# Late chunks in pairs, fewer transposes on TensorE, and seven products for four output blocks of a recurrent attention kernel with an MLP

## The chip, the core and the metric

The kernel runs on one core of a Trainium2 chip. A core has five engines with queues of their own, each in order: TensorE (PE in the profile, its weight loads PEld), VectorE (DVE), ScalarE (ACT), GpSimd (POOL) and SyncE (SP), which here issues nearly all DMAs. TensorE writes to PSUM, eight banks of 128 partitions by 512 float32; the others work between PSUM and SBUF, the on-chip memory of 128 partitions, GpSimd on SBUF alone. The metric is the device time of one execution in microseconds, the median over runs; smaller is better.

## What is computed

Four batches, eight heads, 768 tokens, head size 48. Each head keeps a 48 x 48 state that decays per key channel; the output of all heads (3072 tokens by 384) goes through two matrix products with a leaky ReLU between them.

```python
for t in range(S):
    cur = einsum('bhd,bhe->bhde', u[None] * kt, vt)
    y[:, :, t] = einsum('bhd,bhde->bhe', rt, state + cur)
    state = wt[:, :, :, None] * state + einsum('bhd,bhe->bhde', kt, vt)
x = y.transpose(0, 2, 1, 3).reshape(B * S, H * D)
h = x @ w_in                     # 384 -> 2048
g = np.maximum(0.01 * h, h)
out = g @ w_out                  # 2048 -> 384
```

Inputs and output are float32; the kernel computes its products in bfloat16 with float32 sums.

## The kernel before

The 3072 tokens are 24 chunks of 128. In a chunk the recurrence is made parallel: cumulative sums of log w by a triangular matrix product, their exponentials into r and k (`rk`), both transposed (`rkT`), scores k against r, a mask, masked scores against v, and the state of the previous chunk against r. The bonus with u is r u k summed per head, times v (`vs`). The result y of a chunk is transposed into `xT`, whose columns are the tokens.

The first four chunks are two pairs (function `pair`), 256 tokens each, with two consecutive tokens in one partition, so that a row of a load has 96 floats (per head) instead of 48. The other 20 are single chunks (`single`), each with four loads (L701), a log (L711), one cumulative sum on TensorE (L717) and per-head-pair totals (L720), sums with the log on DVE (L729), exponentials on ACT (L743, L747, L738 for the totals), products on DVE (L405), transposes, scores (L858, eight matmuls that contract over the 48 rows of one head, two heads in the two halves of the array), two masks on DVE (L788), state sums (L798, four matmuls of 96 columns), a scaled state on GpSimd (L775), the new state on DVE (L813), and y: four matmuls from the state (L824) and eight from the masked scores (L829) into one bank, plus the bonus on DVE (L478). `run` takes one or two chunks (`MERGED`) and puts their scores into one step.

A transpose of r and k is either eight matmuls against the identity (L416) with two evacuations on DVE or ACT (L421, L423), or one DMA transpose from SP (`RK_DMA` lists 13 chunks). The transpose of y is three matmuls (L464) and a copy (L469, L471), or a DMA transpose (`Y_DMA` lists 8 chunks).

The MLP goes over blocks of one or two chunks: 16 groups of 128 columns of w_in, three matmuls each (L901), the leaky ReLU on ACT into g (L916, 512 columns at a time), and 16 accumulating matmuls of 384 columns per chunk (L928), a copy on DVE or ACT (L939, L941) and a store (L945).

The order of everything is a written plan. Each step is added to a `Plan` with the engines that may run it, an assumed cost, a priority, the steps it follows and the buffers it reads or takes; `Plan.order` then plays the steps through in assumed time, gives each an engine and a buffer, and the kernel emits the instructions in that order. `RANK` shifts priorities of single steps, `FORCE` fixes engines; limits bound how many PSUM banks a kind of buffer holds at once (`hp` for L901's results 2, `op` for L928's 2). A log must wait until the first L901 step of the chunk `LEAD` before it. In the first 24 us of assumed time gaps of TensorE are filled with matmuls of zeros (L970).

## Time and profile before

| | us |
|---|---|
| runs | 182.0, 183.03, 183.03 |
| median | 183.03 |
| the profiled execution | 181.38 |
| its span, first to last instruction | 179.6 |

The profile comes from that one execution. Busy time of an engine is the union of its instructions; for TensorE the durations of successive matmuls overlap, so one instruction's duration is more than what it adds. The groups of instructions by line give busy time, mean duration in ns of one, and the idle time before them with what ended it. The chain of waits follows the work back from the last instruction to what released it at each step.

The shares of work on TensorE, by line (count, busy us):

| line | what | count | busy us |
|---|---|---|---|
| L901 | x times w_in | 720 | 73.3 |
| L928 | g times w_out | 384 | 73.4 |
| L416 | transposes of r and k | 88 | 7.7 |
| L829 | masked scores times v | 160 | 7.2 |
| L858 | scores | 160 | 6.7 |
| L824 | state into y | 72 | 6.0 |
| L798 | state sums | 64 | 5.3 |
| L464 | transposes of y | 48 | 5.3 |

### The profile page before, as it was taken

Reading aid. Unit: us, or ns where it says so; the run is one execution under the profiler, and the core shown is the slowest. Engines: PE = TensorE matmul, PEld = TensorE weight load, DVE = VectorE, ACT = ScalarE, POOL = GpSimd, SP = SyncE. Lnnn points to the kernel's source line nnn. Section 1 sums busy time; section 2 is a strip of 40 time slices with the busy share of each in tenths; the row PEclk is TensorE's granted clock in tenths of the full one; section 3 lists DMA queues with packets and bytes.
Section 4 is the critical chain, followed back from the end, with each engine's and each line's share of the span. In section 5 each row is a group of like instructions: output and inputs, shape, how many; then the busy total and the mean of one; then the engine's idle time right before and its main releaser. Section 6 shows DMA issues by size and latency. Waiting matters only on the chain.

```text
span 179.6 us, 5197 instructions
## 1 busy us (share of the span) xinstructions
PE 171.6 (96%) x2036; PEld 129.8 (72%) x2037; DVE 115.0 (64%) x231; ACT 115.3 (64%) x253; POOL 102.5 (57%) x138
## 2 busy tenths in 40 slices
PE   7798999999999999999999999999999999999991
PEld 2466888867778788877788767787788786787850
DVE  7699764289789898559677558397468297241102
ACT  2678968855867788884489774485486664652610
POOL 5999632574897686877469854667165665100000
PEclk9999999999999999999999999999999999999998
DMA  5999999998999999999999989999899996600112
GB/s 141 261 283 316 370 376 364 187 199 199 231 191 224 180 229 134 184 213 173 185 181 223 212 179 223 153 215 175 152 254 170 220 163 134 167 9 19 47 44 88
DMA packets 116571, 34.43 MB, mean 192 GB/s; under 512 B 109121, under 2 KB 115778, under 8 KB 116546
## 3 DMA queue, kind: packets, MB, share of 16 engines
q1 hardware_dynamic: 116544, 34.09, 95.8%
q8 instruction: 16, 0.26, 0.7%
q14 instruction: 9, 0.07, 0.1%
q10 hardware_dynamic: 2, 0.00, 0.0%
HBM read 25.17 MB, written 4.72 MB: 166 GB/s over the span
## 4 chain that ended last, share of the span: by engine, by line
PE 77%; DMA 11%; DVE 4%; ACT 2%; issue 2%; SPq 1%; POOL 0%; DVEq 0%; ACTq 0%
PE ps L901 35%; PE ps L928 28%; DMA in<-in_r_dram 3%; DMA in<-in_v_dram 3%; DMA in<-in_w_dram 2%; PE ps L858 2%; DMA xT<-y 2%; PE ps L829 2%; PE ps L717 2%; PE ps L824 2%; PE ps L416 2%; DVE rk L405 2%; PE ps L798 1%; PE ps L464 1%; DVE m L636 1%
## 5 line engine op out<-in xcount | busy, mean ns | idle before, releaser
L901 PE MATMUL ps<-xT,w_in_b 128*128 128x256 bf16 (+1 forms) x720 | 73.3, 251 | 0.4 <-ACT xT L471 0.2
L928 PE MATMUL ps<-w_out_b,g 128*128 128x384 bf16 x384 | 73.4, 326 | 0.0
L916 ACT ACTIVATE g<-ps 128x512 bf16<-128x512 f32 x96 | 56.8, 597 | 25.4 <-PE ps L901 23.2
L901 PEld LDWEIGHTS <-w_in_b 128*128 128x128 bf16 x720 | 57.8, 98 | 9.9 <-issue 0.7
L928 PEld LDWEIGHTS <-g 128*128 128x128 bf16 x384 | 35.2, 98 | 17.3
L405 DVE TENSOR_TENSOR rk<-in,ps 128x384 bf16<-128x384 f32 x46 | 24.5, 548 | 9.9 <-ACT ps L743 6.5
L435 POOL TENSOR_TENSOR ru<-in,ub 128x384 f32<-128x384 f32 x24 | 23.9, 1001 | 9.6 <-DMA in<-in_k_dram 7.6
L788 DVE TENSOR_TENSOR m<-ps,maskb 128x512 bf16<-128x512 f32 x40 | 25.1, 683 | 5.3 <-PE ps L858 5.3
L439 POOL TENSOR_TENSOR ru<-ru,in 128x384 f32<-128x384 f32 x24 | 24.6, 1027 | 3.0 <-DMA in<-in_r_dram 2.4
L775 POOL TENSOR_TENSOR sb<-s,a 128x384 bf16<-128x384 f32 x18 | 15.0, 831 | 16.8 <-ACT a L738 16.8
L447 POOL TENSOR_TENSOR vs<-in,dg 128x384 f32<-128x384 f32 x20 | 16.6, 830 | 9.1 <-DVE dg L443 8.4
L729 DVE TENSOR_TENSOR ci<-ps,lw 128x384 f32<-128x384 f32 x20 | 11.1, 555 | 9.7 <-PE ps L720 4.5
L939 DVE COPY o<-ps 128x384 f32<-128x384 f32 x10 | 5.6, 555 | 15.6 <-PE ps L928 15.4
L443 DVE TENSOR_REDUCE dg<-ru 128x8 f32<-128x384 f32 x24 | 12.9, 544 | 2.1 <-POOL ru L439 2.1
L478 DVE TENSOR_TENSOR y<-ps,vs 128x384 bf16<-128x384 f32 x20 | 11.1, 553 | 3.2 <-PE ps L829 2.6
L455 POOL CAST vb<-in 128x384 bf16<-128x384 f32 x24 | 12.0, 504 | 1.5 <-DMA in<-in_v_dram 1.4
L711 ACT ACTIVATE lw<-in 128x384 bf16<-128x384 f32 x20 | 10.4, 522 | 2.9 <-DMA in<-in_w_dram 2.9
L743 ACT ACTIVATE ps<-ps 128x384 f32<-128x384 f32 x20 | 9.6, 481 | 4.1 <-DVE ci L729 3.6
L738 ACT ACTIVATE a<-ps 64x4 f32<-64x4 f32 x36 | 6.0, 167 | 7.7 <-DVE ci L729 5.1
L813 DVE TENSOR_TENSOR s<-ps,sb 128x384 f32<-128x384 f32 x14 | 7.7, 552 | 3.8 <-PE ps L798 2.7
L747 ACT ACTIVATE ps<-ci 128x384 f32<-128x384 f32 x20 | 9.8, 491 | 0.0
L941 ACT COPY o<-ps 128x384 f32<-128x384 f32 x14 | 6.7, 479 | 4.2 <-PE ps L928 4.0
(90 smaller groups left out, 176.2 us busy)
## 6 DMA issues: line engine op xcount, KB each, us to landing
out_dram<-o SPq DMA_DIRECT2D x24, 192.0 KB, 3.7
in<-in_w_dram SPq DMA_DIRECT2D x20, 192.0 KB, 4.2
in<-in_k_dram SPq DMA_DIRECT2D x20, 192.0 KB, 4.2
in<-in_r_dram SPq DMA_DIRECT2D x20, 192.0 KB, 4.0
in<-in_v_dram SPq DMA_DIRECT2D x20, 192.0 KB, 4.0
in<-in_moe_w_out_dram SPq DMA_DIRECT2D x4, 768.0 KB, 12.1
in<-in_moe_w_in_dram SPq DMA_DIRECT2D x4, 384.0 KB, 6.8
in<-in_moe_w_in_dram SPq DMA_DIRECT2D x2, 768.0 KB, 9.0
```

Of the source, the lines that this page charges most:

```text
L405: (nc.gpsimd if e == "POOL" else nc.vector).tensor_tensor(out=o, in0=x, in1=i, op=ALU.mult)
L435: lambda e: nc.gpsimd.tensor_tensor(out=ru.t[:], in0=kv(), in1=ubv, op=ALU.mult),
L439: lambda e: nc.gpsimd.tensor_tensor(out=ru.t[:], in0=ru.t[:], in1=rv(), op=ALU.mult),
L443: lambda e: nc.vector.tensor_reduce(out=dg.t[:], in_=ru.t[:], axis=AX.X, op=ALU.add),
L447: lambda e: nc.gpsimd.tensor_tensor(out=vs.t[:], in0=vv(), in1=dg.t[:].unsqueeze(2).to_broadcast([128, H, D]), op=ALU.mult),
L455: {"POOL": 0.56}, lambda e: nc.gpsimd.tensor_copy(out=vb.t[:], in_=vv()),
L478: lambda e: nc.vector.tensor_tensor(out=y.t[:], in0=heads(yp.t), in1=vs.t[:], op=ALU.add),
L775: lambda e: nc.gpsimd.tensor_tensor(out=sb.t[:].rearrange("p g a d -> p (g a) d"), in0=s_in.t[:].rearrange("p g a d -> p (g a) d"), in1=a_ ...
L788: lambda e, par=par: nc.vector.tensor_tensor(out=m.t[:, par, :, :], in0=sc[par].t[:].rearrange("p (g t) -> p g t", g=NP), in1=maskb[:].uns ...
L901: nc.tensor.matmul(hp.t[:, a * N : (a + 1) * N], lhsT=w_in_b[:, t, (j + a) * 128 : (j + a + 1) * 128], rhs=xT[:, t, c0 : c0 + N], start=(a ...
L916: lambda e, hp=hp, g=g, j=j, J=J, N=N: nc.scalar.activation(out=g.t[:, j : j + J, 0:N], in_=hp.t[:, 0 : J * N].rearrange("p (a n) -> p a n ...
L928: nc.tensor.matmul(op.t[:, 0:DM], lhsT=g.t[:, j, off : off + 128], rhs=w_out_b[:, j, :], start=(j == 0), stop=(j == NJ - 1))
```

## The change

Three parts of the program change, and with them every constant of the plan.

**Late chunks in pairs.** `single` and `run` give way to `late`, which takes two consecutive chunks of one batch (256 tokens) with two tokens per partition, for all 20 late chunks. Ten pairs have four loads each (L910), half as many as before and twice as large. Both cumulative sums come from one product of two matmuls (L936) and two operations on DVE (L956, L961); the totals of both 64-token halves and parities take eight matmuls of two columns (L941). Partition p of a pair holds tokens 2p and 2p + 1, so its lower and upper 64 partitions are the two chunks. Scores (L1053), state sums (L1034) and state into y (L1059, function `inter`) are matmuls in 64 x 64 quarters of the array; the masked sums (L1059, `intra`) in 64-row halves. The state is kept as 64 + 64 rows by 4 x 48 (192 elements per partition instead of 384), and is passed on inside a pair as well.

```diff
+            def sums(e):
+                for g in range(NP):
+                    for js in range(2):
+                        for x in range(len(pps)):
+                            q = slice(64 * x, 64 * x + 64)
+                            for par in range(2):
+                                nc.tensor.matmul(
+                                    pps[x].t[64 * par : 64 * par + 64, g * D : (g + 1) * D],
+                                    lhsT=rk2.t[q, js, 1, 2 * g + par, :], rhs=vbs[js].t[q, 2 * g + par, :],
+                                    start=(g == 0 and js == 0), stop=(js == 1), skip_group_check=True)
...
+            s_sc = step(
+                {"PE": 0.73 if first else 0.78}, row(inter(1), scores), P0 + 1, deps=[*s_T, *s_used], reads=[rkT2, *used],
+                takes=[*(sc for js in range(2) for sc in scs[js]), *yps[first:]])
...
+            s_yi = step(
+                {"PE": 0.83 + 0.26 * len(more)}, row(intra, inter(0), *(x["sums"] for x in more)), P0 + 2,
+                deps=[*s_ms, *s_vbs, *s_T, *s_used, *(y for x in more for y in x["deps"])],
```

So one step of TensorE holds half of the state products and all scores, and a second one the masked sums, the other half, and the state sums of the next pair; it follows all four masks (L1129). The bonus is scaled on GpSimd in four instructions of 64 partitions (L1021) instead of two of 128; one cast of v per pair may go to ACT.

Tokens of a late chunk lie in `xT` with the even ones first. The leaky ReLU puts them back, by writing every second column of g:

```diff
+                def leaky(e, hp=hp, g=g, j=j, J=J, N=N, c0=c0):
+                    o, i = g.t[:, j : j + J, 0:N], hp.t[:, 0 : J * N]
+                    if c0 < B:
+                        i = i.rearrange("p (a n) -> p a n", a=J)
+                    else:
+                        i = i.rearrange("p (a x t) -> p a t x", x=2, t=64) if N == L else i.rearrange("p (s x t) -> p s t x", x=2, t=64)
+                        o = o.rearrange("p a (t x) -> p a t x", x=2) if N == L else o.rearrange("p a (s t x) -> p (a s) t x", x=2, t=64)
+                    nc.scalar.activation(out=o, in_=i, func=AF.Prelu, alpha=0.01)
```

**Transposes.** Seven pairs transpose r and k by DMA (two each), three on TensorE (L598, 16 matmuls a pair); seven pairs transpose y by one DMA each, three on TensorE (L649).

```diff
-    RK_DMA = {6, 11, 12, 14, 15, 16, 17, 18, 19, 20, 21, 22, 23}
-    Y_DMA = {8, 10, 16, 17, 20, 21, 22, 23}
-    MERGED = {6, 10, 12, 14, 16, 18, 20}
-    LEAD = 4
-    AHEAD = 4
+    RK_DMA = {8, 12, 14, 16, 18, 20, 22}
+    Y_DMA = {8, 10, 12, 14, 16, 18, 20}
+    LIMITS = {"hp": 4, "op": 4, "op2": 1, "cp": 2, "ek": 4, "yy": 2, "warm": 1, "warm2": 1}
+    LAST = [(0, 256), (256, DM)]
+    LEAD = 6
+    AHEAD = 7
+    SEVEN_LAST = 6
-    blocks = [2, 1, 1, 1, 1, 2, 2, 2, 2, 2, 1, 1, 2, 2, 2]
+    blocks = [2, 1, 1, 1, 1, 2, 2, 2, 2, 1, 2, 2, 2, 2, 1]
```

**Seven products.** In the two-chunk blocks among the last six (four blocks) g W_out is cut in 2 x 2: two chunks of rows, even and odd groups of 128 inner rows, two halves of 192 columns. Strassen's method in Winograd's form makes the four results from seven products of halves, each of eight matmuls of 192 columns (L1251), instead of eight products. DVE makes four sums of parts of g per block (L1234, 1024 elements per partition), once four differences of parts of w_out (L1203, `mix`, 1536 elements), and the sums of the products come from accumulation in PSUM, three copies (L1265, L1267) and five additions (L1272) of 192 columns per block.

```diff
+                for name, o, in0, in1, op in (
+                    ("s1", lambda: sv(0), lambda: a(1, 0), lambda: a(1, 1), ALU.add),
+                    ("s3", lambda: a(1, 0), lambda: a(0, 0), lambda: a(1, 0), ALU.subtract),
+                    ("s2", lambda: sv(1), lambda: sv(0), lambda: a(0, 0), ALU.subtract),
+                    ("s4", lambda: sv(2), lambda: a(0, 1), lambda: sv(1), ALU.subtract),
+                ):
...
+            plain = [(px, lambda: a(0, 0), lambda: qs[:, 0, 0]), (py, lambda: a(0, 1), lambda: qs[:, 1, 0])]
+            third = [(pv, lambda: a(1, 0), lambda: tp(2))]
...
+            s_6 = products(8.5, b1, [(px, lambda: sv(1), lambda: tp(1))], [*s_sum["s2"], s_mix[1], s_e1])
+            s_4 = products(10.5, b3, [(pz, lambda: a(1, 1), lambda: tp(3))], [s_mix[3], *dict.fromkeys(g_done)], start=True, stop=True)
+            s_5 = products(12.5, b1, [(px, lambda: sv(0), lambda: tp(0))], [*s_sum["s1"], s_mix[0], s_e2], stop=True)
+            s_3 = products(14.5, b2, [(pw, lambda: sv(2), lambda: qs[:, 1, 1])], [*s_sum["s4"], s_7], stop=True)
```

The other blocks keep the plain products (L1319 for w_in, L1353 for w_out); the very last chunk's output is made in 256 and 128 columns.

**The plan.** Buffers may take several neighbouring places of a pool; the plan knows which PSUM bank is being read or written, and counts TensorE's early steps double. `RANK` has 986 entries instead of 144 and `FORCE` other engines, so the order of nearly every step moves. In the built order a w_in load stands first on SP's queue, ahead of the first w; the last products of the last two-chunk block are emitted after those of the last single block. The masks and evacuations of the two early pairs are the same operations, with some of them on another engine.

1057 lines of the change are left out of this document (655 added, 402 removed), and 136 rows, old and new, of the table RANK.

## The prediction

> **What bounds the kernel now.** I read the page first: how busy the engines are, and what the chain that ended last consists of.
>
> ```profile
> span 179.6 us, 5197 instructions
> ...
> PE 171.6 (96%) x2036; PEld 129.8 (72%) x2037; DVE 115.0 (64%) x231; ACT 115.3 (64%) x253; POOL 102.5 (57%) x138
> ...
> PE 77%; DMA 11%; DVE 4%; ACT 2%; issue 2%; SPq 1%; POOL 0%; DVEq 0%; ACTq 0%
> ```
>
> TensorE (PE) is busy 96% of the span, no other engine over 64%. Next PE's waits (total us, times, longest) and the chain of waits in order of time:
>
> ```profile
> PE ps L970 <- DVE zeros L278: 1.3, 1, 1.3
> PE ps L416 <- DVE rk L405: 0.5, 1, 0.5
> ```
> ```profile
> 17.08 0.50 ACT y L680
> 17.59 0.64 ACT rkT L423
> 18.22 0.74 ACT xT L471 x2
> 19.00 1.47 PE ps L901 x12
> ...
> 170.71 5.21 PE ps L928 x32
> 176.00 0.56 DVE o L939
> ```
>
> The longest waits are 1.3 us, at the very start, and 0.5 us; none is on a DMA. So there are three stages: up to 19.00 loads and short steps end in a ScalarE chain; from 19.00 to 176.00 matmuls follow each other; then 3.6 us of copy and store. In the middle stage only PE's work counts, and as the distance from start to start, since durations overlap. The timeline gives these prices (start, us covered, group, count):
>
> ```profile
> 10.86 0.64 PE L624 MATMUL ps<-rkT 48*64 48x128 bf16 x32
> ...
> 14.33 0.57 PE L649 MATMUL ps<-vb,m 64*128 64x48 bf16 x32
> ...
> 25.72 1.50 PE L901 MATMUL ps<-xT,w_in_b 128*128 128x128 bf16 x24
> 27.06 0.81 PE L928 MATMUL ps<-w_out_b,g 128*128 128x384 bf16 x4
> ```
> ```profile
> 100.61 0.81 PE L928 MATMUL ps<-w_out_b,g 128*128 128x384 bf16 x4
> 101.26 0.82 PE L901 MATMUL ps<-xT,w_in_b 128*128 128x256 bf16 x6
> 101.92 0.81 PE L928 MATMUL ps<-w_out_b,g 128*128 128x384 bf16 x4
> ...
> 105.61 0.81 PE L928 MATMUL ps<-w_out_b,g 128*128 128x384 bf16 x4
> 106.36 0.62 PE L858 MATMUL ps<-rkT 48*128 48x128 bf16 x16
> 106.91 0.82 PE L928 MATMUL ps<-w_out_b,g 128*128 128x384 bf16 x4
> ...
> 108.88 0.33 PE L824 MATMUL ps<-sb,rkT 128*128 128x96 bf16 x4
> 109.05 0.36 PE L829 MATMUL ps<-vb,m 128*128 128x48 bf16 x8
> 109.25 1.46 PE L928 MATMUL ps<-w_out_b,g 128*128 128x384 bf16 x8
> ```
>
> With 384 columns a matmul takes 0.65/4 = 0.1625 us, with 256 0.65/6 = 0.109, with 128 1.34/24 = 0.056, with 96 0.17/4 = 0.0425, with 48 0.20/8 = 0.025. The four L928 before the scores (L858) take 0.75 instead of 0.65: going from whole-array matmuls to 64-row ones costs 0.10, and coming back another 0.10, so 16 scores cost 0.45 + 0.20. The last matmul of a group hangs over by 0.16 to 0.17 (0.36 covered, 0.20 to the next start). Without that, 32 in four 64x64 tiles (L624) take 0.47, 0.0147 each, a quarter of 0.056; 32 in two 64-row tiles (L649) 0.41, 0.0128 each, half of 0.025. Tiles side by side do run side by side.
>
> **The change part by part, on PE.** *Seven products.* Of the last six blocks four have 256 tokens. Each had 32 matmuls of 384 columns, 5.2 us; it gets 56 of 192 columns. None of 192 is in the trace; halfway between 128 and 256 lies 0.0825, so 4.62. Four times -0.58 is **-2.3 us**. Splitting the last chunk's output in 256 and 128 columns costs 16 x (0.109 + 0.056 - 0.1625) = +0.04.
>
> *Transposes.* Late r,k transposes on PE: before 7 chunks x 8, after 3 pairs x 16; -8 x 0.056 = **-0.45**. y: before 12 late chunks x 3, after 6 x 3: -18 x 0.056 = **-1.0**. Despite the change's words PE gets fewer; the DMA queue carries as many r,k (14 for 13) and 7 wider y for 8.
>
> *Late chunks in pairs.* Before: scores with their switches, 7 double groups at 0.65 and 6 single at 0.43, 7.1; masked sums (L829) 160 x 0.025 = 4.0; state sums (L798) 64 and state into y (L824) 72, each at 0.0425, 5.8; totals 72 x 0.025 = 1.8: 18.7 us. After: scores 320 x 0.0147 = 4.7; masked sums 320 x 0.0128 = 4.1; totals 80 x 0.025 = 2.0; state sums 256 and state into y 288, in 64x64 tiles with 48 columns; and in the built order 52 changes of tile form for 26, 52 x 0.10 = 5.2 (ten of them lead from one tiled form to the other, which no row shows: 0 to 0.10 each, taken as the others). The 544 small ones are in no trace: from below 0.025/4 = 0.0063 each, 3.4 us, from above the 0.0147 of the 128-column ones in the same tiles, 8.0. I take 3.4, because L624 has the very tile form and shows all four tiles at once. Sum 19.4: **+0.7**, up to +5.3. Here a rule speaks against the change. The Trainium skill, TensorEngine Tiling (Array Packing), Restrictions, says that column tiling gives up the fast weight load; and TensorE: Matmul & The Clock Gate, LDWEIGHTS, prices a load at its columns over 1.2 GHz. By these an estimate is 64/1.2 = 53 ns for a load, 13.3 ns for each of the 544 with four tiles side by side, 3.8 us more than I take; L624, whose matmuls are as long as such a load, fits both.
>
> PE together: -2.3 + 0.04 - 0.45 - 1.0 + 0.7 = **-3.0 us**. The first 384-column cumulative sums and all L901 work stay.
>
> **Off PE.** *VectorE (DVE).* Rows for it:
>
> ```profile
> L788 DVE TENSOR_TENSOR m<-ps,maskb 128x512 bf16<-128x512 f32 x40 | 25.1, 683 | 5.3 <-PE ps L858 5.3
> ...
> L405 DVE TENSOR_TENSOR rk<-in,ps 128x384 bf16<-128x384 f32 x46 | 24.5, 548 | 9.9 <-ACT ps L743 6.5 <-ACT ps L747 2.4 <-ACT ps L543 0.8
> ```
>
> A late pair's masked sums, its state into y and the next pair's state sums are one step on PE, which now waits for four masks, 4 x 0.683 = 2.7 us; before, a single chunk waited for two. Behind it in PE's queue stand the L1319 and L1353 of the blocks. Between scores and this step the built order puts 3.1 to 3.3 us of matmuls in five of the ten pairs (five groups of 0.65) and over 4 in the others. That covers the masks with 0.4 to 0.6 to spare, so nothing; with one 0.55 product in front of them in each of the five about +0.5 in all, with two about +3. The other new wait: per seven-product block DVE makes four sums of 1024 elements and five additions of 192 columns. By the product of 384 a sum lies between 0.73 (at half the price per element, with half the bytes) and 1.46. In the last block the third product needs two sums behind a ScalarE step of 0.60 to 0.78: 2.1 to 3.7. PE has meanwhile 24 x 0.056 + 16 x 0.0825 + 8 x 0.056 + 4 x 0.109 = 3.5 us of other matmuls: covered but for 0.2; without the cover up to 3.7, once. In all DVE gets 4 x (2.9 to 5.8 + about 2) and four 1536-element differences of 1.1 to 2.2, 24 to 40 on its 115 us: still below PE.
>
> *ScalarE.* Late chunks now hold tokens in the order even, odd; the activation L1339 writes every second column of g. What that costs shows in the pairs' evacuations, where r goes to every second column (17.45) and k does not (15.02):
>
> ```profile
> 15.02 0.59 ACT L423 COPY rkT<-ps 128x512 bf16<-128x512 bf16 x1
> ...
> 17.45 0.77 ACT L423 COPY rkT<-ps 128x512 bf16<-128x512 bf16 x1
> ...
> 19.86 0.60 ACT L916 ACTIVATE g<-ps 128x512 bf16<-128x512 f32 x1 [0.18 <-PE ps L901]
> ```
>
> So 80 of 96 activations take between 0.60 and 0.78: 0 to 14 us more on an engine with 64 us free. PE has twice the PSUM banks for them (hp 4 for 2), so I take nothing.
>
> *Loads.* 80 loads of 192 KB become 40 of 384 KB with rows twice as long. PE waits for none, so nothing. *Start.* A w_in load of 393,000 bytes goes ahead of the first w on SP's queue. The first 10 us moved 207 GB/s (last number of their row):
>
> ```profile
> 0.00:10.00 10.00, 7.53 (x53) 3.85 (x55) 7.25 (x27) 4.93 (x9) 7.95 (x22) 1.00 0.96 207
> ```
>
> So w, k, r and v come up to 1.9 later. Against that, of the two y and xT copies one of each goes to DVE, instead of all one after the other on ACT (17.08 to 18.96): -0.50 - 0.37 and part of the 0.64 between. -1.2 to +1.9; I take 0. *End.* The last copy (0.56) becomes an addition of half the columns, about 0.36: **-0.2**.
>
> **Sum.** -3.0 - 0.2 = -3.2: the span of 179.6 becomes 176.4. The profiled execution took 181.38, its span plus 1.8; the median of the three runs is 183.03, so 183.0 - 3.2 = **179.8 us**.
>
> **The rivals.**
> - *More than that:* the start gets 1.2 shorter and the holes in PE's stream (0.5 us and less each, about 1 in all) close. 177.6. For it: the ACT chain before 19.00. Against: the load put first.
> - *The new tile form eats it:* the 544 cost 0.0147 each, +4.6: 184.4, within 1% of before. For it: no row has so short matmuls in that form. Against: L649 halves at 48 columns what L829 costs. The Trainium skill's rule on weight loads, quoted above, would give much the same, 183.6.
> - *ScalarE becomes late, slower than before:* each late activation takes 0.17 more, 14 us, in an in-order queue with the exponentials that the next pair's chain needs. PE stops at L1319 for a bank, or at the scores. If half lands on PE, -3.2 + 7 = +3.8: 186.8. It decides from 5 us of the 14, a third. For it: the 0.77 above. Against: (115.3 + 14)/176 is 73%.
>
> **Numbers.** Under 1% (1.8 us) no measurement of this kernel tells from no change. Chances: my forecast 0.53, more 0.22, tile form 0.13, ScalarE 0.12. Faster by over 1% (below 181.2) takes nearly all of the first, since half of the doubtful 4.6 would be needed to leave it, and the second: 0.70. Same takes most of the third and a little of the first: 0.17. Slower takes the fourth and a rest of the third: 0.13. The range runs from 175.6 (the second, with the ten changes between tiled forms at nothing, -1.0, and 1.0 for the spread of the three runs, 182.0 to 183.03) to 184.6, which holds the third, and leaves out ScalarE's case and the ends.
>
> **What would show it.** Right: seven-product groups of eight at 0.66 us; four or five gaps of 0.10 per late pair; 32 state sums in about 0.2; first L1319 near 19; PE's last matmul ending near 172.9; L1339 near 0.60. Wrong: waits of PE on ACT g or DVE m of over 3 us in all, the 64x48 groups at 0.4 and more, or a first L1319 after 20.5.

## The result and the profile after

| | before | after |
|---|---|---|
| runs, us | 182.0, 183.03, 183.03, 183.27 | 184.89, 185.87, 185.33, 184.88 |
| median, us | 183.03 | 185.11 |
| the profiled execution, us | 181.38 | 184.89 |
| its span, us | 179.6 | 182.8 |

The ratio is 1.015, with a 95% interval of 1.011 to 1.019: the changed kernel is slower by 1.5%, where 1.8% faster was forecast, and 185.1 lies outside the range that ended at 184.6.

First the page of the changed kernel: its span, how busy each engine is, and the engines' shares of the chain that ended last.

```profile
span 182.8 us, 6793 instructions
...
PE 173.0 (95%) x2860; PEld 136.7 (75%) x2860; DVE 130.4 (71%) x276; ACT 111.1 (61%) x226; POOL 110.2 (60%) x151
...
PE 52%; DVE 3%; ACT 2%; issue 1%; DVEq 0%; ACTq 0%
```

PE is still what counts, with 824 more matmuls and only 1.4 us more busy time. How that divides is seen in the three stages, cut at the first up product (L901, now L1319) and at the end of PE's last matmul. The windows of before, then of after (stretch, its length, busy time and count of PE, PEld, DVE, ACT, POOL, granted clock, DMA share, GB/s):

```profile
0.00:19.00 19.00, 15.41 (x225) 9.35 (x227) 15.51 (x43) 12.32 (x26) 15.82 (x31) 1.00 1.05 257
19.00:175.91 156.91, 156.15 (x1811) 120.48 (x1810) 98.96 (x188) 103.02 (x228) 86.70 (x107) 1.00 0.97 186
175.91:179.60 3.69, 0.00 (x0) 0.00 (x0) 0.56 (x1) 0.00 (x0) 0.00 (x0) 0.81 0.29 107
```
```profile
0.00:22.36 22.36, 17.85 (x246) 10.46 (x247) 16.68 (x48) 13.07 (x28) 19.20 (x40) 1.00 0.98 271
22.36:179.27 156.91, 155.12 (x2614) 126.28 (x2614) 113.28 (x228) 98.04 (x199) 91.02 (x112) 1.00 0.86 183
179.27:182.80 3.53, 0.00 (x0) 0.00 (x0) 0.39 (x2) 0.00 (x0) 0.00 (x0) 0.89 0.40 149
```

The middle stage is as long as it was, 156.91 us. All that was lost, 3.36 us, was lost before the first up product. The timeline of that first stage, of before and then of after (start, us covered, engine, line, operation, names, count; in brackets the idle time before it and what ended that):

```profile
3.44 0.65 DVE L385 TENSOR_TENSOR o<-o 1x384 f32<-1x384 f32 x1
...
4.58 0.84 ACT L502 ACTIVATE lw<-in 128x768 bf16<-128x768 f32 x1 [1.97 <-DMA in<-in_w_dram]
...
5.18 0.56 DVE L399 COPY ub<-ps 128x384 f32<-128x384 f32 x1 [0.41 <-PE ps L392]
...
5.48 0.48 PE L510 MATMUL ps<-lw,tstr 128*128 128x384 bf16 x2
...
6.28 1.96 POOL L435 TENSOR_TENSOR ru<-in,ub 128x384 f32<-128x384 f32 x2
```
```profile
5.75 1.92 POOL L494 TENSOR_SCALAR_AFFINE_SELECT maskp<-maskp 64x64 bf16<-64x64 bf16 x8
...
6.34 0.92 PE L1398 MATMUL ps<-zeros 128*128 128x512 bf16 x5
6.54 0.48 ACT L583 COPY ub<-ps 128x384 f32<-128x384 f32 x1 [3.35 <-PE ps L574]
6.91 0.85 ACT L696 ACTIVATE lw<-in 128x768 bf16<-128x768 f32 x1
...
7.81 0.48 PE L705 MATMUL ps<-lw,tinc 128*128 128x384 bf16 x2 [0.55 <-ACT lw L696]
...
7.91 0.82 POOL L540 CAST w_in_b<-in 128x768 bf16<-128x768 f32 x1
...
8.70 1.95 POOL L619 TENSOR_TENSOR ru<-in,ub 128x384 f32<-128x384 f32 x2
...
13.30 0.64 PE L835 MATMUL ps<-rkT 48*64 48x128 bf16 x32
...
22.36 0.81 PE L1319 MATMUL ps<-xT,w_in_b 128*128 128x256 bf16 x6 [0.23 <-ACT s L820]
```

The log of w starts 2.33 later, and so do the first cumulative sums (5.48 to 7.81); the first scores are 2.44 late (10.86 to 13.30), the first up product 3.36. What stands in front is to be seen on four queues at once. On SP's, the w_in load; w is in SBUF at 6.61 instead of 4.56. On ScalarE's, the copy of u (L583, on VectorE before), ahead of the log. On PE's, the last of the three matmuls that spread u, with steps of VectorE between them (L385 before, L567 now), comes at 6.17 instead of 4.82, and behind it stand five warm-ups. On GpSimd's, the eight selects of the new mask, 1.92 us, and a cast of w_in, ahead of the first bonus (its k is in SBUF at 8.08 instead of 6.07). Of the 2.33 of the log, w accounts for 2.05 and the copy of u for the other 0.28.

In the middle I added up every start-to-start distance of PE. At the prices per matmul the work fell from 151.4 to 147.0 us. But changes of tile form rose from 3.1 to 6.1, and waits from 2.0 to 3.6: -4.4 + 3.0 + 1.6 = +0.2, nothing within what the split allows (where a change of form and a wait fall together, some 0.2 can be put down to either). PE's timeline of after near 71 us shows the new prices, and there and further on four of the waits:

```profile
70.67 0.31 PE L1059 MATMUL ps<-sb,rkT 48*64 48x48 bf16 x16
70.81 0.47 PE L1034 MATMUL ps<-vb,rk 64*64 64x48 bf16 x32
71.22 0.83 PE L1319 MATMUL ps<-xT,w_in_b 128*128 128x256 bf16 x6
72.23 2.20 PE L1319 MATMUL ps<-xT,w_in_b 128*128 128x256 bf16 x18 [0.18 <-DVE rk L587]
...
84.81 0.81 PE L1319 MATMUL ps<-xT,w_in_b 128*128 128x256 bf16 x6 [0.31 <-ACT g L1339]
...
124.98 0.31 PE L1059 MATMUL ps<-sb,rkT 48*64 48x48 bf16 x14 [0.24 <-DVE rk L587]
...
133.07 2.78 PE L1319 MATMUL ps<-xT,w_in_b 128*128 128x256 bf16 x24 [0.40 <-DVE y L1153]
```

Sixteen state products take 0.14 to the next group, 0.0088 each; 32 state sums take 0.41 to the next up product, and without 0.10 for the change of form 0.0097 each. Over the whole trace it is 0.0087 and 0.0100. The six up products at 71.22 last 0.65 and the next group starts at 72.23, so 0.36 is lost there, waiting for r and k decayed (L587).

The groups of the other engines, of after:

```profile
L1339 ACT ACTIVATE g<-ps 128x512 bf16<-128x512 f32 x96 | 54.5, 601 | 31.7 <-PE ps L1319 27.4 <-PE ps L1251 2.9
...
L1272 DVE TENSOR_TENSOR o<-ps,o 128x192 f32<-128x192 f32 x20 | 6.7, 354 | 6.7 <-PE ps L1251 4.6 <-ACT o L1267 2.0
...
L1234 DVE TENSOR_TENSOR in<-g 128x1024 bf16<-128x1024 bf16 x4 | 3.0, 756 | 1.1 <-ACT g L1339 1.0
```

The leaky ReLU with every second column takes 601 ns, where it took 597. VectorE's sums of 1024 elements take 0.67 to 0.69 us, but for one of 0.95 that is in the group shown. That these sums made an input of PE late is not to be seen: p0 below does without them and has the same waits.

### The profile page after: what moved, and what is told of

It is laid out like the page before. It is cut to its first block, busy times and chain, and to the rows that moved or that the text cites. A ratio compares the mean times of both kernels' runs of the same rounds, so it can differ in the third digit from the quotient of the medians.

```text
span 182.8 us, 6793 instructions
## 1 busy us (share of the span) xinstructions
PE 173.0 (95%) x2860; PEld 136.7 (75%) x2860; DVE 130.4 (71%) x276; ACT 111.1 (61%) x226; POOL 110.2 (60%) x151
## 4 chain that ended last, share of the span: by engine, by line
PE 52%; DVE 3%; ACT 2%; issue 1%; DVEq 0%; ACTq 0%
PE ps L1319 22%; PE ps L1353 12%; PE ps L1251 10%; PE ps L1059 4%; PE ps L1053 2%; PE ps L936 1%; ACT ps L965 1%; PE ps L1034 1%; DVE ci L961 1%; DVE ci L956 1%; DVE rk L587 1%; PE ps L941 1%; DVE o L1272 0%; ACT g L1339 0%; DVE y L1153 0%
## 5 line engine op out<-in xcount | busy, mean ns | idle before, releaser
L1319 PE MATMUL ps<-xT,w_in_b 128*128 128x256 bf16 (+1 forms) x720 | 70.9, 251 | 1.1 <-DVE y L1153 0.4
L1319 PEld LDWEIGHTS <-w_in_b 128*128 128x128 bf16 x720 | 57.5, 98 | 8.2 <-issue 1.5
L1353 PE MATMUL ps<-w_out_b,g 128*128 128x384 bf16 (+2 forms) x272 | 47.3, 317 | 0.0
L1021 POOL TENSOR_TENSOR vs<-in,dg 64x384 f32<-64x384 f32 x40 | 33.7, 841 | 16.2 <-DVE y L1153 11.7
L1353 PEld LDWEIGHTS <-g 128*128 128x128 bf16 x272 | 24.7, 98 | 12.7
L587 DVE TENSOR_TENSOR rk<-in,ps 128x384 bf16<-128x384 f32 x46 | 23.7, 547 | 6.0 <-ACT ps L741 3.5
L1129 DVE TENSOR_TENSOR m<-ps,maskp 128x512 bf16<-128x512 f32 x40 | 25.1, 681 | 3.3 <-PE ps L1053 2.8
L1153 DVE TENSOR_TENSOR y<-ps,vs 128x384 bf16<-128x384 f32 x20 | 10.4, 549 | 4.5 <-issue 1.9
L956 DVE TENSOR_TENSOR ci<-ps,lw 128x384 f32<-128x384 f32 x10 | 5.6, 555 | 10.8 <-PE ps L941 9.7
L1272 DVE TENSOR_TENSOR o<-ps,o 128x192 f32<-128x192 f32 x20 | 6.7, 354 | 6.7 <-PE ps L1251 4.6
L1366 ACT COPY o<-ps 128x384 f32<-128x384 f32 (+1 forms) x11 | 5.1, 461 | 10.5 <-PE ps L1353 10.4
L1398 PE MATMUL ps<-zeros 128*128 128x512 bf16 (+1 forms) x41 | 9.3, 351 | 1.7 <-DVE zeros L456 1.7
L1251 PEld LDWEIGHTS <-g 128*128 128x128 bf16 x128 | 10.6, 98 | 0.3
L1093 POOL TENSOR_TENSOR sb<-s,a 128x192 bf16<-128x192 f32 x16 | 8.7, 548 | 3.3 <-DVE s L1097 1.9
L640 POOL CAST vb<-in 128x384 bf16<-128x384 f32 x14 | 7.6, 557 | 3.2 <-PE ps L1059 3.0
L923 ACT ACTIVATE lw<-in 128x768 bf16<-128x768 f32 x10 | 8.5, 853 | 0.0
L961 DVE TENSOR_TENSOR ci<-ps,lw 128x384 f32<-128x384 f32 x10 | 5.6, 556 | 3.9 <-ACT ps L965 2.4
L1251 PEld LDWEIGHTS <-in 128*128 128x128 bf16 x96 | 8.2, 98 | 0.2
```

The costliest lines, as they stand in the source:

```text
L587: (nc.gpsimd if e == "POOL" else nc.vector).tensor_tensor(out=o, in0=x, in1=i, op=ALU.mult)
L1021: lambda e, x=x, j=j, q=q, dg=dg: nc.gpsimd.tensor_tensor(out=vs2[x].t[64 * j : 64 * j + 64], in0=view("v", j)()[q], in1=dg.t[q].unsqueeze ...
L1129: lambda e, par=par, js=js: nc.vector.tensor_tensor(out=ms[js].t[:, par, :, :], in0=scs[js][par].t[:].rearrange("p (g t) -> p g t", g=NP), ...
L1153: lambda e, y=y, x=x: nc.vector.tensor_tensor(out=y.t, in0=heads(yps[x].t), in1=vs2[x].t[:], op=ALU.add),
L1251: nc.tensor.matmul(o(), lhsT=x()[:, i, :], rhs=y()[:, i, :], start=fresh, stop=(stop and i == ii[-1]), skip_group_check=True)
L1319: nc.tensor.matmul(hp.t[:, a * N : (a + 1) * N].rearrange("p (s n) -> p s n", n=L), lhsT=w_in_b[:, t, (j + a) * 128 : (j + a + 1) * 128], ...
```

## The experiments

Two theories went in. START: the loss comes from the queues of the first 22 us, and goes as they are cleared. MIDDLE: the gain is eaten in the middle stage, by changes of form, small matmuls and waits, and clearing the start brings little. All edits are to the changed kernel, except r1 to r3, which are to the kernel before. After `PLAN = plan` in the changed kernel the list `order` holds the steps by number; 124 is the first w_in load, 125 its cast on GpSimd, 5 the copy of u, 12 the first cumulative sums, 146 an early step on GpSimd. A ratio stands against the kernel before on the same chip. "First up" is the start of the first up product in the profiled execution, and "rest" that execution's time minus first up. In the runs from s1 on the kernel before has medians of 181.6 to 182.4, not 183.03, so between rows the ratio says more than the time.

| run | median, us | ratio (95%) | first up | rest |
|---|---|---|---|---|
| before | 183.03 | | 19.00 | 162.4 |
| after | 185.11 | 1.015 (1.011-1.019) | 22.36 | 162.5 |
| s1_load_behind | 185.80 | 1.024 (1.021-1.026) | 22.10 | 163.4 |
| s2_u_on_dve | 185.10 | 1.020 (1.017-1.023) | 22.85 | 162.5 |
| s3_both | 185.84 | 1.023 (1.020-1.026) | 22.84 | 163.4 |
| s4_start | 185.92 | 1.023 (1.017-1.028) | 22.59 | 163.1 |
| s5_start_more | 183.67 | 1.011 (1.008-1.013) | 21.50 | 162.2 |
| s7_start_all | 183.28 | 1.009 (1.008-1.011) | 21.32 | 161.9 |
| s8_start_waits | 184.04 | 1.013 (1.010-1.015) | 22.01 | 163.1 |
| s9_banks | 185.60 | 1.018 (1.015-1.020) | 22.40 | 163.6 |
| s10_banks_row | 185.13 | 1.016 (1.013-1.019) | 21.19 | 163.4 |
| s11_fewer_warm | 182.32 | 1.004 (1.001-1.007) | 21.28 | 162.4 |
| s12_filled | 182.23 | 1.004 (1.002-1.005) | 20.46 | 161.8 |
| a1_filled | 185.16 | 1.019 (1.017-1.022) | 22.34 | 163.4 |
| d1_between | 188.06 | 1.034 (1.031-1.038) | 22.85 | 165.4 |
| d2_ahead | 185.76 | 1.022 (1.019-1.025) | 22.86 | 162.9 |
| p0_plain | 188.14 | 1.036 (1.033-1.038) | 22.89 | 164.9 |
| r1_load_first | 183.26 | 1.008 (1.005-1.011) | 21.80 | 161.8 |
| r2_start_of_after | 183.06 | 1.007 (1.004-1.010) | 21.77 | 161.5 |
| r3_filled | 182.27 | 1.003 (1.002-1.005) | 20.54 | 161.6 |

**One queue at a time.** s1 puts the w_in load behind the loads of the first pairs, into a buffer of its own, and its cast further back; s2 puts the copy of u on VectorE; s3 does both; s4 adds the selects, a load of v and two casts at later places.

```diff
+    first_in = pool.tile([128, 2, DM], F32, name="first_in")
+        plan.steps[124][5][0].t = first_in[:]
+        for i, j in [(124, 122), (125, 610)]:
+            order.remove(i)
+            order.insert(order.index(j), i)
```
```diff
+        plan.eng[5] = 'DVE'
```
```diff
+        plan.steps[124][5][0].t = first_in[:]
+        plan.eng[5] = 'DVE'
+        for i, j in [(124, 122), (125, 610), (67, 124), (92, 93), (91, 93)]:
+            order.remove(i)
+            order.insert(order.index(j), i)
...
+            if i == 146:
+                pair_masks()
```

> The changed kernel, with the first w_in load (and its POOL cast) moved behind the eight loads of the two early pairs; nothing else moves. Theory START (the 3.4 us by which the first up product came later, 22.36 against 19.00, are lost in the start and are the whole slowdown; several delays lie there one behind the other): w lands near 4.6 instead of 6.6, but the log L696 stands behind the copy of u on ScalarE, which ended at 7.02, so it still begins near 6.9; the later loads of r, v and the second pair land 1 to 2 us sooner and POOL loses a cast of 0.82 us. First up 0.5 to 1.5 us sooner, near 21.3, and the median near 184.0 (183.4 to 184.6). Rival MIDDLE (the end is set by the loads or the late attention, so that a sooner start comes back as waits later): the first up moves, the time stays at 184.9 to 185.4.

> The changed kernel, with only the copy of u from PSUM moved from ScalarE to VectorE, which is idle from 6.1 to 9.2 us. START: the log L696 then waits for w, which lands at 6.6, so it begins near 6.65 instead of 6.91: 0.2 to 0.3 us, median near 184.9. MIDDLE: no difference either. If the copy by itself were the cause, the log would begin near 4.6 and the time fall by 2.

> Both edits together: the w_in load behind the two pairs and the copy of u on VectorE. START: now the log begins near 4.7, as before the change (4.58), and the steps behind it come about 2 us sooner, until POOL holds them back (its eight selects for the pair masks, 1.92 us, still stand in front of its first ru). First up near 20.3 (19.8 to 21.2), median near 183.1 (182.6 to 184.0), so more than the two edits by themselves add up to. MIDDLE: first up near 20.3 and the time still 184.9 to 185.4, with 2 us more of waits behind it.

> As the kernel with both edits, and POOL relieved: the eight selects of the pair masks stand behind the first weights' casts (near 30 us) instead of in front of everything, the load of the second pair's v goes last of the eight, and the two casts of the second pair's v stand behind the first pair's own casts and bonus. START: the casts of v are ready 1 to 2 us sooner, PE's wait for the intra products and the ScalarE wait of 2.2 us near 16.8 behind it go; first up 19.0 to 19.8, as before the change, and the median 181.9 (181.4 to 182.8). MIDDLE: time 184.9 to 185.4 whatever the first up.

None of the four won anything. Taken alone, that would speak for MIDDLE. The timeline of s4 says otherwise:

```profile
4.52 0.84 ACT L699 ACTIVATE lw<-in 128x768 bf16<-128x768 f32 x1 [1.34 <-DMA in<-in_w_dram]
...
6.15 0.48 PE L577 MATMUL ps<-o,ones_f 128*128 128x384 bf16 x1 [0.20 <-DVE o L570]
...
6.43 1.70 PE L1408 MATMUL ps<-zeros 128*128 128x512 bf16 x5
...
7.92 0.84 PE L708 MATMUL ps<-lw,tinc 128*128 128x384 bf16 x2
```

The log is back at 4.52, as early as before, but the sums that use it start at 7.92, later than in the changed kernel. They now wait in PE's own queue, for the spread of u, which waits for VectorE, and for five warm-ups behind it. So the obstacles stood one behind the other, and each, when taken away, uncovered the next. PE's rate does not hide a gain here, though in s2, s3 and s4 it became full (full price, in the words of the expectations) only near 10 us, as the last section shows: d1, d2 and p0 below have the changed kernel's start with the same late rate, and their first up product comes at 22.85 to 22.89, that of s2, s3 and s4 at 22.85, 22.84 and 22.59. In s1 the cast that was moved back made a new one, in the second group of up products:

```profile
22.10 0.81 PE L1320 MATMUL ps<-xT,w_in_b 128*128 128x256 bf16 x6 [0.24 <-ACT s L821]
...
24.14 0.83 PE L1320 MATMUL ps<-xT,w_in_b 128*128 128x256 bf16 x6 [0.95 <-POOL w_in_b L541]
```

**All of them.** s5 also puts the fills of VectorE that nobody needs yet behind the splits of u, one warm-up instead of five ahead of the first sums, and the cast of w_in and a cast of v at other places. s7 refines it: only the `rk` buffers of the first pair are filled early, and the casts of v and w_in and a few steps of GpSimd are in another order.

```diff
-        for t in pools["lw2"] + pools["rk"]:
+        for t in pools["lw2"]:
...
+        for i, j in [(124, 122), (125, 100), (67, 124), (92, 93), (91, 93), (33, 42)]:
...
+            if i == 4:
+                more_fills()
...
-                    gap = s - pe_free - 0.1
+                    gap = s - pe_free - 0.1 if i != 12 else 0.5
```

> The four runs before showed that behind the first up product the trace is rigid (157 us to PE's last product, whatever was moved), and that their first up did not come sooner, though w landed at 4.5 and the log began at 4.52: the first cumulative sums L708 then stood on PE behind the spread of u (its last part at 6.15) and five warm-up products (6.43 to 8.13), and began at 7.92 against 5.48 before the change. This kernel adds to the last of them: VectorE's 1.15 us of fills of rk and the fills of the pair masks stand behind the two splits of u, one warm-up product in the place of five stands in front of the first cumulative sums, the second cast of v stands on POOL before the product that waits for the sums dg, and the POOL cast of the first w_in piece before the two last bonus products. START, as it stands now (no single edit; the first up waits at the end of a row of queues, u on VectorE, then PE, then ScalarE, POOL and DVE, and comes sooner only when all of them are relieved): first cumulative sums near 5.6, scores near 11.3, first up 20.0 to 20.8, and the time falls by as much, to 182.5 to 183.7 where the changed kernel has 185. Rival: the first up is held by something that none of these edits touches (the landing of r and k of the second pair, POOL's 2 us products): first up 22 or later and the time 185 or more. Rival MIDDLE: first up 20 to 21 and the time still 185.

> The run before moved the first up product from 22.36 to 21.50 us and the time from 185.1 to 183.7, nearly one for one. This kernel relieves the queues that its trace shows next: VectorE fills only two of the eight rk buffers ahead of the copy of u (which ended at 7.86, with POOL waiting for it), so POOL's first ru begins near 6.9 instead of 7.95; the w_in piece of the first up product is loaded in front of the second pair's r and v and cast in ScalarE's idle stretch near 13.7; POOL makes the second pair's product of r (PE waited 0.70 for it) ahead of the casts of v2, whose sums stand later on PE; the y transposes of the first pair stand on PE in front of the second pair's last two key transposes. START: first up 19.7 (19.2 to 20.6) and the time falls with it, to 182.3 (181.6 to 183.0), 2.5 under the changed kernel. Rival: PSUM holds it (the second pair's cumulative sums need banks that the four masks free one after the other, from 12.2 on): first up stays at 21 to 21.5 and the time at 183.2 to 183.7.

Now it moves. In s5 the first sums start at 6.28, the scores at 11.63, the first up product at 21.50, and the ratio is 1.011, where s4, its nearest relative, has 1.023. Part of the distance from s4 is the rate; the changed kernel's profiled execution had full rate from 6.3 us, as s5 has, and against that one the first up product gains 0.86. In s7 it is 21.32, held by the second pair: its scores (20.68) wait for the PSUM bank of its state sums (18.66), and six warm-ups stand at 19.11 between the two. START holds, for the part that came back.

s9 gives those sums bank 7, moves four steps of PE in the start and four late products, s10 besides changes the order of ScalarE and VectorE steps near 70 us, s11 keeps bank 7, two of the moves in the start and three of the late ones, and ends the warm-ups at 16 us of the plan.

```diff
+        plan.steps[101][5][0].t = pools["ps"][7]
```
```diff
-    WARM_UNTIL = 24.0
+    WARM_UNTIL = 16.0
```

> The kernel with the relieved start, and two things more. In its trace the second pair's scores (20.68) and the first up product (21.32) stood behind the second pair's sums, whose PSUM bank the scores needed; here one of the two banks of those sums is another one that is free by then, and scores and first up stand ahead of the addition that waits for VectorE. START: first up 20.3 (19.8 to 20.9), 1.0 us sooner. In the middle, of the six products that were moved ahead of a waiting step only those stay where the wait did not come back (the one near 84 us, the two near 124), and an up product is moved ahead of the one that waited .56 near 132: 0.5 to 1.3 us. Together 181.9 (181.2 to 182.6); if the waits are the late chain's own and come back, 182.3 to 182.8.

> The same, and for the pair near 70 us another order on VectorE and ScalarE: ScalarE's two readings of the bank of the cumulative sums (decay and first exponential) come one after the other ahead of VectorE's two, in the place of taking turns with them, and the state's addition and one product of r stand ahead of a y addition that nothing waits for. If the waits near 70 and 74 us (0.35 to 0.65 and 0.44) come from these turns: 0.4 to 0.9 us less than the run beside it. If PE would there wait for the same engine's next result: within 0.2 us of it, or more.

> The changed kernel with the relieved start, the other bank for the second pair's sums, the three moved products that helped (the waits near 84 and 124 us were gone with them), and no warm-up products planned behind 16 us. START: scores near 19.7, first up 20.3 to 20.7, middle 156.9 less 0.9 to 1.1 us of waits: time 181.6 to 182.6, under the changed kernel by 2.5 to 3.5 and within 1 us of the kernel before. Rival: without warm-up products PE's clock falls in the gaps near 17 to 20 us and first up or the first up products come late: 183 or more.

s9 and s10 were misses that the edit itself made. The gaps are planned, and where a step was moved the program saw a longer gap and filled it. The timeline of s9 at its first up product:

```profile
20.09 1.74 PE L1421 MATMUL ps<-zeros 128*128 128x512 bf16 x7
...
22.40 0.82 PE L1329 MATMUL ps<-xT,w_in_b 128*128 128x256 bf16 x6
23.22 1.89 PE L1421 MATMUL ps<-zeros 128*128 128x512 bf16 x8
```

That first up is 22.40 in s9 and 21.19 in s10 has another reason: the first scores are already 1.22 apart (12.42 and 11.20), and PE's rate was full from 7.6 us in the one and 5.9 in the other. The other order near 70 us won nothing, the middle stages last 158.36 and 158.43 us.

Without these warm-ups, s11 comes to 1.004 (its profiled execution, 183.67, was the slowest of ten). s12 is s11 with two warm-ups of 256 columns between the three steps of the spread of u, and a1 the changed kernel with 512, 512 and 256 columns in the same gaps and nothing else.

```diff
+                for n in [[], [512, 512], [256]][x]:
+                    nc.tensor.matmul(warm.t[:, 0:n], lhsT=zeros[:, 0:128], rhs=zeros[:, 0:n], start=True,
+                                     stop=True, skip_group_check=True)
```

> The relieved start with fewer planned warm-up products and the three moved products, with one warm-up product of 256 columns in each gap of the spread of u: half price until about 5 us instead of 7.0. First up 20.2 to 20.8 in the profiled execution instead of 21.28, time 181.9 (181.3 to 182.4), level with the kernel before (181.6) and 3 us under the changed kernel. If the half price does not depend on these gaps: 182.3, with the same two groups.

> The changed kernel with warm-up products in the two gaps of the spread of u (4.6 to 5.5 and 5.9 to 6.2 us). Its profiled execution had full price from 6.3 us on, and its queues were late all the same, so QUEUES: the time stays at 184.6 to 185.2 and only the executions near 185.9 go (they would be those with half price until 10 us). CLOCK alone as the cause: 183 or less.

The timeline of s12:

```profile
4.26 0.71 DVE L577 TENSOR_TENSOR o<-u_row 128x384 f32<-128x384 f32 x1 [0.97 <-DMA u_row<-in_u_dram]
...
4.47 0.84 ACT L709 ACTIVATE lw<-in 128x768 bf16<-128x768 f32 x1 [1.29 <-DMA in<-in_w_dram]
...
6.24 0.49 PE L718 MATMUL ps<-lw,tinc 128*128 128x384 bf16 x2
...
11.59 0.64 PE L848 MATMUL ps<-rkT 48*64 48x128 bf16 x32
...
20.46 0.82 PE L1332 MATMUL ps<-xT,w_in_b 128*128 128x256 bf16 x6
```

s12 is 2.9 us faster than a1 on the same chip (182.23 against 185.16); its late code differs from a1's by the three moved products. Of the 3.36 us of late start 1.90 are back. The other 1.46 stand in two places by the rows: 0.76 ahead of the first sums (6.24 against 5.48) and 0.73 between the first scores and the first up product (8.87 against 8.14). The first has a candidate that no run took away: the load of u is issued at 1.37 instead of 0.80, behind a fill of all 128 rows of its tile, and VectorE's first step on it begins at 4.26 instead of 3.44. The second was not settled. No version beat the kernel before. In a1 the slow executions did not go, as had been expected: two of its four runs are 185.42 and 185.76, the latter the profiled one, with the stall of 1.54 that the last section shows.

**From the other side.** r1 gives the kernel before the w_in load first; r2 also the copy of u on ScalarE ahead of the log, and eight selects on GpSimd; r3 is r1 with three warm-ups ahead of the first sums.

```diff
+        order.remove(118)
+        order.insert(order.index(6), 118)
```
```diff
+            if i == 13:
+                for n in (512, 512, 512):
```

> The kernel before, with its first w_in load moved to the head of SyncE's queue, as the change does; nothing else. The prediction gave this up to 1.9 us and set it against 1.2 us of other things. START: w lands near 6.5 instead of 4.56, the log begins there instead of at 4.58, and all that follows comes 1.5 to 2 us later: first up 20.5 to 21.0 instead of 19.0, the time 1.5 to 2.0 us over the kernel before. Rival (the start has slack in POOL and VectorE that takes the load in): first up within 0.7 us of 19.0 and the time within 0.7 us of the kernel before.

> The kernel before with three things that the change put into the start: the w_in load first, the copy of u on ScalarE ahead of the first log, and the eight selects of the pair masks (1.9 us, into a tile that nothing reads) on POOL in front of its first products. START: POOL's first ru begins near 8.2 instead of 6.28 and the steps add up where POOL is late too: first up 21 to 22.4, time 2.0 to 3.4 us over the kernel before, most of the 3.4. Rival: no more than with the load alone.

> The kernel before with the w_in load first, and three more warm-up products of 512 columns in front of the first cumulative sums, where PE stood idle from 6.15 to 7.10 us. If the late end of the half price (13 us in the run without them) was what made that run slow, and the idle time kept it going: full price from 6 to 8 us on, first up near 20.5 (20.0 to 20.9) instead of 21.80, and the time 181.6 to 182.4, so that the load by itself costs 0.2 to 0.8 us. If the load is what costs: first up 21.5 or later, time 183.2 as before.

The timelines of r1, then of r3:

```profile
6.20 0.84 ACT L502 ACTIVATE lw<-in 128x768 bf16<-128x768 f32 x1 [3.59 <-DMA in<-in_w_dram]
...
7.10 0.80 PE L510 MATMUL ps<-lw,tstr 128*128 128x384 bf16 x2 [0.95 <-ACT lw L502]
...
11.84 0.63 PE L416 MATMUL ps<-ident,rk 128*128 128x128 bf16 x4
```
```profile
6.08 0.84 ACT L502 ACTIVATE lw<-in 128x768 bf16<-128x768 f32 x1 [3.45 <-DMA in<-in_w_dram]
...
7.21 0.85 PE L510 MATMUL ps<-lw,tstr 128*128 128x384 bf16 x2
...
9.58 0.40 PE L416 MATMUL ps<-ident,rk 128*128 128x128 bf16 x4
```

The load alone moves the log from 4.58 to 6.20, and the first up product by 2.80. About half of that, 1.26, goes with the three warm-ups of r3: in r1 PE stands idle for 0.95 ahead of the first sums and runs at half its rate until about 13 us (four transposes cover 0.63 instead of 0.40), in r3 until about 9. So the load by itself costs at most 1.54 in first up and 0.3% in the ratio, and the lost rate another 0.5% (eight of r1's ten runs are 183.16 or more and all twelve of r3's 182.82 or less; the other two of r1, 181.53 and 181.65, are as fast as the kernel before, and were not profiled). Nor is a late start paid in full there: r3's middle stage lasts 156.11 us instead of 156.91, as waits of the kernel before near 48, 53 and 89 us are gone. r2 adds nothing to r1: behind the late load the copy of u and the selects are covered. In the changed kernel's profiled execution the rate is not the cause: it is full from 6.3 us on, and a1, full from 6.7, starts its first up product at 22.34 all the same. Where the same start ran at half rate until about 10 (d1, d2, p0), that cost 0.5 more.

**The middle.** d1 puts a 128 x 128 product of zeros between the two halves of the scores of each late pair, so two changes of form more for each; d2 puts the same product ahead of them, where PE comes from whole-array work anyway. p0 makes the four seven-product blocks plain, with the ranks of the steps that remain.

```diff
+                    if js == 1:
+                        nc.tensor.matmul(scs[1][1].t[:, 0:128], lhsT=zeros[:, 0:128], rhs=zeros[:, 0:128], start=True, stop=True, skip_group_check=True)
```
```diff
-    SEVEN_LAST = 6
+    SEVEN_LAST = 0
```

> The changed kernel with one product more in each of the ten late pairs, 128 rows by 128 columns of zeros, between the two halves of the 64x64-tile scores: it costs its own .056 us and, by the trace's gaps, a switch to the full form and one back (.145 and .09 to .10). If switches cost what the gaps say and lie on PE's path: 10 x (.056 + .24) = 3.0 us more, of which 2.4 are the switches. If the gaps only show the end of a form's pipeline, which the next products would have waited for anyway, or if PE has slack there: 0.6 us or less.

> The control: the same product of zeros ten times, but ahead of each late pair's first 64x64 product, where PE comes from a full form already, so that no switch is added. 10 x .056 = 0.6 us more than the changed kernel (0 to 1.0). The difference between this run and the one with the product in between is the price of 20 switches: 2.4 us by the gaps, 0 if switches are free.

> The changed kernel with plain products in the four late blocks of 256 tokens in the place of the seven products of halves (the order of the steps before 120 us is the same; the plain products stand where the seven stood). By PE's prices: 128 products of 384 columns at .1625 = 20.8 us in the place of 224 of 192 at .0827 = 18.5, so 2.3 us more, 187.4 (186.6 to 188.2), if VectorE's sums and differences (4 x 4 x .7 = 11 us, and 5 for the mixed weights) cost nothing on the path, as predicted. If they do (VectorE busy at the late waits near 124 and 132 us): less than 1 us more, or none.

d1 less d2 is 2.30 us for 20 changes, 0.115 each by the medians; by the middle stages of the two profiled executions, 159.77 and 157.31, less the stall of 0.43 that d1 has near 73 us, 0.10 each. In p0 the middle stage lasts from 22.89 to 182.04, 159.15 us, against 156.91: the seven products win 2.24 us, and PE's waits stand at the same places, with the same lengths to within 0.1 us, as in the changed kernel. Both parts of MIDDLE have their forecast sizes; what is left for it are the small matmuls and the waits.

s8 is s7 with six products moved ahead of steps of PE that wait (the last six of the list; the others are those of s7).

```diff
+        for i, j in [(122, 66), (124, 130), (125, 100), (67, 124), (33, 42), (97, 88), (92, 98), (91, 98), (101, 103), (102, 103), (59, 89), (62, 89), (123, 77), (60, 87), (678, 270), (694, 698), (714, 367), (711, 728), (814, 541), (800, 541)]:
```

> The same start, and on PE six products of g with the weights moved one place ahead of the step that waited in the trace of the changed kernel (the waits near 55.6, 71.8, 74.2, 84.2 and 124 us, together 2.1 us): nothing is computed otherwise. If these waits are single late inputs, which a product that is ready can cover: 1 to 2 us less than the kernel with the start alone, 181.0 (180.3 to 182.0). If the late pairs' chain sets the rate there (cumulative sums, ScalarE's exponentials, VectorE's products, each waiting for the one before), the wait comes back one step later: less than 0.5 us gained.

The waits near 84 and 124 us went, but one for g near 56 grew to 0.60, that for y near 133 stayed at 0.40, and the median is 0.76 above that of s7. By the profiled executions the moves neither won nor lost: 0.69 of the distance is the first up product (22.01 against 21.32), where the start is the same and PE's rate became full near 7 instead of 6 us, and the middle stage is 0.92 longer, with a stall of 1.30 where s7 has one of 0.47 (last section). That a wait covered in one place comes back in another is what the waits near 56 and 133 suggest, not more.

## Why the prediction was wrong

**The step that failed is *Start*** ("So w, k, r and v come up to 1.9 later ... -1.2 to +1.9; I take 0"). It came to +3.36, beyond its upper bound: as much as the whole slowdown, and half of the distance from the forecast. The load's part was sized nearly rightly (w, k, r and v are 2.05, 2.01, 1.94 and 1.76 later; r1 and r3 show up to 1.54 of it in first up). Three things were not in the sum: the copy of u ahead of the log on ScalarE, PE's own queue with the later spread of u and the five warm-ups ahead of the first sums, and the eight selects on GpSimd. No single one of the four queues decides, as s1 to s4 show; clearing all of them, and the warm-ups ahead of the second pair's scores, gave back 1.90 (s12). What each is worth is not shown, and r2 shows the copy and the selects to cost nothing behind the load in the kernel before. And the gain set against it, one copy of y and of xT moved to VectorE, stood in a stretch, from the first scores to the first up product, that had become 0.92 longer (9.06 against 8.14). The prediction named the signs to look for: a first up product after 20.5, and groups of 32 state sums at 0.4 and more, which measured 0.41.

**The late attention was sized too low.** The 544 matmuls in 64x64 tiles with 48 columns were taken at 0.0063 and measured 0.0087 and 0.0100, 5.05 us in all instead of 3.43: +1.6. The true value lies between the row chosen and the other bound (0.0147). The estimate of 0.0133 by the Trainium skill's rule, TensorE: Matmul & The Clock Gate, LDWEIGHTS, is not borne out by these rows. "The new tile form eats it" was a third right.

**New waits were taken at 0 and measured +1.6.** The four masks were indeed covered, no wait for m is in the trace. What PE waits for are other new ends of the pair's chain: the state (L1097), the decayed r and k (L587), y (L1153) and g. The prediction priced the wait that it could name and put the others at what they were; that it is the chain of two chunks at a time which makes them is argued from the names, no run took it away. Its rival of closing holes had the sign wrong.

**Right in size:** seven products, -2.3 forecast, -2.24 by p0. Transposes of r,k and y, -1.45 forecast; by the start-to-start sums L416 and L464 took 5.46 and L598 and L649 take 4.08, -1.38. A change of form, 0.10 taken, 0.10 to 0.115 by d1 and d2, +3.0 for all where 2.6 was meant. The strided activation, 601 ns, so ScalarE's rival fell. The end, -0.2 forecast, 3.69 to 3.53. VectorE's new sums, differences and additions take some 23 us where 24 to 40 were forecast, its sums of 1024 elements costing 0.67 to 0.69 (one 0.95), under the low bound of 0.73; as other work fell, its total rose by 15.4.

The balance in us: from the forecast -3.2, the start adds 3.4, the small matmuls 1.6, the waits 1.6 and the form changes 0.4; the other groups came out 0.4 cheaper. That makes +3.4, and the span went from 179.6 to 182.8, +3.2; the rest is the rounding of the terms. Outside the span the profiled execution took 2.1 instead of 1.8.

## What to carry to other kernels

Where a change reorders a start, follow each queue from its first instruction to the first product of the main stage, and price the sum of what stands in front, not the one item that the change is about; removing the items one by one can show nothing until the last is gone. See in each trace at which rate PE ran there before two starts are compared. When a main stage keeps its length to 0.01 us though its work fell by 4.4, look for the gain in changes of form and new waits, by start-to-start distances. And a program that fills planned gaps will fill the ones that an experiment makes.

## What the runs showed of the hardware

**PE's rate in the first microseconds is not in the granted clock.** In r1 two matmuls of 384 columns cover 0.80 at 7.10, and four transposes 0.63 at 11.84; the same groups cover 0.48 and 0.40 in the kernel before. Yet the granted clock of r1's page shows nine tenths or more in every slice but the last. The change to full rate came near 5 us in the kernel before, between 5 and 6 in the changed one, near 7 in s8, s9 and s11, near 9 in r3, near 10 in s2, s3, s4, d1, d2 and p0, and near 13 in r1 and r2. With the changed kernel's own start it came once between 5 and 6 and three times near 10 (d1, d2, p0). Where PE's gaps ahead of the first sums were filled (a1, s12) it came before 7, but so it did unfilled in s1, s5, s7 and s10. The Trainium skill, TensorE: Matmul & The Clock Gate, Part 1: The HAM clock gate, states that TensorE runs at half its clock until a free-running window of some 3.4 us has been busy, and that the same kernel can change at different times. These runs agree on the half and on the different times; they do not show the length of a window.

**A change of tile form costs 0.10 to 0.12 us** (d1 against d2, 20 changes). The Trainium skill, TensorEngine Tiling (Array Packing), Tiling Modes, states that a change of mode drains TensorE, without a price; the runs agree and give one.

**A wait that nothing in the profile ends.** In the late pair near 71 us PE stood still inside a group of small matmuls in some profiled executions: 0.20 in s2, 0.47 in s7, 1.22 in s11, nothing in the changed kernel or s12, and in the rows of d1, s8 and a1:

```profile
72.76 0.18 PE L1061 MATMUL ps<-sb,rkT 48*64 48x48 bf16 x1 [0.43 <-issue]
```
```profile
72.38 0.24 PE L1069 MATMUL ps<-sb,rkT 48*64 48x48 bf16 x5 [1.30 <-issue]
```
```profile
72.49 0.18 PE L1062 MATMUL ps<-sb,rkT 48*64 48x48 bf16 x1 [1.54 <-issue]
```

Nothing that the group needs was late by the profile. The stall does not lengthen the time by all of itself, as waits behind it shrink (a1's middle stage is 0.87 longer than the changed kernel's, with a stall of 1.54), but the rest column of the table is to be read with it in mind. The traces point to PE's own instructions. In all six executions the stall ends at the same place of PE's list, with 2240 to 2242 recorded matmuls and weight loads behind it, whatever group that falls in, and 1.33 to 1.62 us after a 16 KB packet on the queue that the page calls q8, instruction, has ended. In the ten traces of the changed kernel and its variants without the stall, PE came to that place 1.39 us or more after that packet. So much the sixteen traces have in common; no run changed it, and the cause stays open.
